# Attention with a decay, then a gated FFN: the decay rows issued from ScalarE's DMA queue, and the first 480 tasks of the order rewritten

## The chip, the core and the metric

The kernel runs on one core of one Trainium2 chip. The core has four engines that compute (TensorE or PE, VectorE or DVE, ScalarE or ACT, GpSimd or POOL) and SyncE or SP, which here issues DMAs only. Each engine works through its own instructions in order and waits on semaphores for the others. The metric is the device time of one execution in microseconds; lower is better. The time before is the median of 3 runs.

## What is computed

The reference is forgetting attention over 8 batches of 8 heads, sequence 576, head size 64, followed by a gated convolutional FFN (512 to 1024 and back):

```python
def _attn_ref(q, k, v, f):
    scores = scale * np.matmul(q, k.transpose(0, 1, 3, 2))
    cum = np.cumsum(np.log(np.clip(f, 0.0001, 1.0)), axis=-1)
    decay = cum[:, :, :, None] - cum[:, :, None, :]
    scores = np.where(causal, -1000000000.0, scores + decay)
    attn = np.exp(scores - np.max(scores, axis=-1, keepdims=True))
    attn = attn / (np.sum(attn, axis=-1, keepdims=True) + 1e-09)
    return np.matmul(attn, v)

def _moe_ref(x, w_in, conv_w, w_out):
    h = np.maximum(x @ w_in, 0.0)
    ...
        conv_out += conv_w[k][None, None, :] * hp[:, k:k + S, :]
    gate = 1.0 / (1.0 + np.exp(-conv_out))
    return h * gate @ w_out
```

All inputs and the output are float32.

## The kernel before

**Units.** The attention runs in 16 half batches of four heads, hb 0 to 15; the FFN runs in 8 batches, b 0 to 7, each after its two half batches. A half batch's Q and K stand transposed in one of four tiles `qk` (in the rows of the order `qk_85` to `qk_88`, for hb modulo 4). The heads' dimensions are read as 16-bit halves, so every other row of such a tile is free, and into some of these free rows go the decay terms: the cumulated logarithms of f, which then enter the scores through the same matmul. For hb 0 the decay comes in by matmuls of its own instead. For hb 1 to 7 two small DMAs, `rows_of` (L200 to L204, 4.5 and 9 KB), copy the decay rows from a DRAM tile `image` into the qk tile. The image itself is written once, by three DMAs from the decay tile `kc` (`decay_image`, L278). For hb 8 to 15 `fill` writes all free rows by three larger DMAs.

**Tasks.** The kernel adds some thousand named tasks, each with its engine, its predecessors and the buffers that it takes and gives, and then plays them in the order of one long string, ORDER (L18). Within an engine the instructions stand in the order of that string. `name@ENGINE` picks an engine where a task may run on several. The names that matter here, with hb or b and a further index:

- `dca dcl dcs dck`: the decay (DVE, ACT, DVE, DVE); `ki`: the image; `rwN`: the decay rows of hb N ("pair N" below, as it is two DMAs); `zc`: constants of the image.
- `ld`, `tp`, `cl`: Q and K of hb 0 and 1 loaded plainly, turned on PE and copied into the qk tile with the free rows cleared. `qN.0`, `qN.1`: Q and K of hb N from 2 on, loaded by a transposing DMA (L180); `clN.x` then clears the free rows on DVE, up to hb 7.
- `vB.k`: the five loads of V for batch B (L210); `vaN.x`: casts to 16 bits. `wi`, `wo`, `wic`, `woc`: the FFN's weights staged in four buffers `ob` and cast.
- `sdI`, `soI.s`, `stN`: scores on PE (diagonal, off the diagonal, tail; I is 2N or 2N+1); `ed`, `eo`, `et`: their exponentials on ACT; `pvN.u`: times V on PE; `n`, `m`: normalising on DVE; `tN`, `txN`: turned on PE and copied.
- `fB.x`, `rB.x`, `cB.x`, `dB.x`, `aB.x`, `gB.x`: FFN chunk x of batch B: first matmul (PE), relu (ACT), convolution in two steps (DVE), gate function (ACT), gating (DVE). `oB.c`: second matmul; `eB.a`, `sB.a`: result copied out of PSUM and stored.

**Buffers.** PSUM holds four tiles `ps`; each score, FFN or turning task on PE takes one, and the task on ACT or DVE that reads it gives it back. So PE can be at most four such tasks ahead of ACT and DVE.

**DMAs.** Each DMA, of SP and ACT alike, raises one of eight semaphores when it has landed. In the rows of the built order they are called `DMAHW0_49` to `DMAHW7_49`; they are dealt out in turn over the DMAs of both engines, about in the order of the string. A DMA whose semaphore has been used before waits for the DMA that used it last, besides what it needs. What stands in `[waits ...]` behind a row names the semaphores that the row waits for. Before the change ACT issues three DMAs (f twice, and the convolution's weights), all at the start; the image and the pairs are SP's, among the loads:

```python
add("ki", "SP", ["dck"], lambda: decay_image("SP"))
add(f"rw{hb}", "SP", [f"cl{hb}.{side}" for side in range(2)] + ["ki"], lambda hb=hb: rows_of(hb))
```

Of the kernel before, what the change touches and what calls it, by code (L numbers as in the profile page):

```python
# [56 lines left out]
def kernel(  # L57
# [17 lines left out]
    BH = B * H  # L75
# [7 lines left out]
    HS = HH * S  # L83
# [16 lines left out]
    image = dpool.tile([4, 2, BH, S], BF16, name="image")  # L100
# [45 lines left out]
    add = plan.add  # L146
# [53 lines left out]
    def rows_of(hb):  # L200
        h0 = 2 * PAIRS if hb == 0 else 0
        c = slice(hb * HH + h0, (hb + 1) * HH)
        nc.sync.dma_start(even_rows(hb, 0, 1, h0 * S, HS), image[0:1, 0, c, :].rearrange("j h s -> j (h s)"))
        nc.sync.dma_start(even_rows(hb, 1, 2, HS + h0 * S, 2 * HS), image[1:3, 1, c, :].rearrange("j h s -> j (h s)"))  # L204
# [73 lines left out]
    def decay_image(e):  # L278
        for j, a, h in ((0, 0, 0), (1, 1, 0), (2, 1, 1)):
            {"SP": nc.sync, "POOL": nc.gpsimd}[e].dma_start(image[j, a], kc[BH * h:BH * (h + 1)])  # L280
# [411 lines left out]
```

## Time and profile before

| what | value |
|---|---|
| median of 3 runs | 246.28 us (245.67 to 247.3) |
| the profiled execution | 246.53 us, its span 244.8 us |
| granted TensorE clock | 0.999 |
| DMA moved | 49.68 MB, mean 203 GB/s |

The profile is of one execution. Its page gives busy time and share of the span for each engine, the chain of work that ended last, followed back from the last instruction, and the costliest groups of instructions. Views of the trace give the same for stretches of the span, the instructions in order of time, and who waited for whom. In a line of the order in time the first two numbers are the start and the length in us; what stands in square brackets is the idle time of the engine ahead of it and what ended it. Lines of "SPq" and "ACTq" are DMA issues: they show the time that issuing took, not when the data landed. `L` numbers are lines of the kernel.

The DMA queue is in use from the start nearly to the end: the queue of SP carries 48.97 of the 49.68 MB in 120085 packets, and the page's mean busy share of the core's 16 DMA engines is 0.9 or more in most of the first 28 of its 40 slices.

### The profile page before, as it was taken

What the parts mean: (1) busy time and instruction counts of PE and PEld (TensorE: products, weight loads), DVE (VectorE), ACT (ScalarE), POOL (GpSimd) and SP (SyncE); (2) the same over time, 40 slices, a digit from 0 to 9 for tenths busy, and PEclk for the clock granted to TensorE, in tenths of its full rate; (3) what the DMA queues carried; (4) which work ended last, traced back from release to release, by engine and by line L of the source; (5) the groups of instructions that cost most, each with busy time, mean ns of one, the idle gap of its engine ahead of it and who ended that gap; (6) DMA issues with size and microseconds to landing.
All of it is one profiled execution on the core that took longest, in us unless ns stands there. A gap on an engine that the chain in (4) does not pass through costs nothing.

```text
span 244.8 us, 6395 instructions
## 1 busy us (share of the span) xinstructions
PE 226.9 (93%) x2627; PEld 145.2 (59%) x2627; DVE 205.9 (84%) x323; ACT 206.8 (84%) x278; POOL 51.5 (21%) x77
## 2 busy tenths in 40 slices
PE   0899799779989999999999999999999999999991
PEld 0787585557555676575556765685575566444440
DVE  5635359999998999999999979996999889999941
ACT  2768677999989899999999999999988996798442
POOL 8020520004220030022311580165302221000000
PEclk9999999999999999999999999999999999999999
DMA  7999999999899999999999999969997870541426
GB/s 189 333 162 243 289 212 197 196 249 260 187 178 177 222 162 246 252 297 208 195 251 264 202 189 274 263 144 186 240 255 192 210 165 3 146 162 58 163 86 214
DMA packets 120280, 49.68 MB, mean 203 GB/s; under 512 B 109863, under 2 KB 110375, under 8 KB 120251
## 3 DMA queue, kind: packets, MB, share of 16 engines
q1 hardware_dynamic: 120085, 48.97, 89.7%
q8 instruction: 20, 0.33, 0.6%
q10 hardware_dynamic: 166, 0.31, 0.4%
q14 instruction: 9, 0.07, 0.1%
HBM read 21.11 MB, written 10.17 MB: 128 GB/s over the span
## 4 chain that ended last, share of the span: by engine, by line
PE 80%; DVE 8%; DMA 6%; issue 1%; ACT 1%; POOL 1%; ACTq 1%; SPq 0%; DVEq 0%
PE ps L475 25%; PE ps L430 21%; PE ps L313 15%; PE ps L390 7%; PE ps L395 3%; PE ps L166 2%; PE ps L415 2%; PE ps L321 2%; DMA pd<-in_moe_conv_w_dram 2%; DMA ob<-in_moe_w_out_dram 2%; DVE u L447 2%; DVE u L449 2%; DMA qk<-image 2%; DVE hg L459 1%; DVE qk L186 1%
## 5 line engine op out<-in xcount | busy, mean ns | idle before, releaser
L430 PE MATMUL ps<-xt,w_in_f 128*128 128x512 f16 (+1 forms) x512 | 69.9, 286 | 0.0
L371 ACT ACTIVATE pp<-ps 128x1024 f16<-128x1024 f32 x64 | 64.8, 1033 | 4.4 <-PE ps L313 2.8
L475 PE MATMUL ps<-w_out_f,hg 128*128 128x512 f16 x288 | 66.9, 379 | 0.7 <-POOL w_out_f L519 0.7
L313 PE MATMUL ps<-qk 128*128 128x128 bf16 (+2 forms) x576 | 63.4, 240 | 1.6 <-DMA qk<-image 0.8
L447 DVE SCALAR_TENSOR_TENSOR u<-ht,cwt 128x576 f32<-128x576 f16 x64 | 53.3, 849 | 3.2 <-ACT ht L441 3.2
L452 ACT ACTIVATE hg<-u,cw 128x576 f16<-128x576 f32 x64 | 48.7, 784 | 5.9 <-DVE u L449 5.8
L449 DVE SCALAR_TENSOR_TENSOR u<-ht,cwt,u 128x576 f32<-128x576 f16 x64 | 53.1, 844 | 0.5
L430 PEld LDWEIGHTS <-w_in_f 128*128 128x128 f16 x512 | 34.4, 98 | 28.5
L313 PEld LDWEIGHTS <-qk 128*128 128x128 bf16 x576 | 39.2, 98 | 19.8 <-issue 3.0
L441 ACT ACTIVATE ht<-ps 128x576 f16<-128x576 f32 x64 | 40.9, 663 | 6.2 <-DVE hg L459 3.1
L475 PEld LDWEIGHTS <-hg 128*128 128x128 f16 x288 | 26.9, 98 | 29.7 <-issue 0.9
L459 DVE SCALAR_TENSOR_TENSOR hg<-hg,ht 128x576 f16<-128x576 f16 x51 | 39.0, 776 | 0.5 <-ACT hg L452 0.5
L357 POOL TENSOR_SCALAR_AFFINE_SELECT pp<-pd 128x1024 f16<-128x1024 f32 x16 | 19.7, 1244 | 51.7 <-ACT pd L354 51.7
L390 PE MATMUL ps<-va,pp 128*128 128x65 f16 x640 | 24.8, 193 | 1.0 <-DVE va L218 1.0
L390 PEld LDWEIGHTS <-pp 128*128 128x128 f16 x640 | 22.5, 97 | 3.5 <-DVE va L218 1.3
L406 DVE TENSOR_TENSOR xm<-ps,rc 128x896 f16<-128x896 f32 (+1 forms) x32 | 23.9, 751 | 0.5
L354 ACT ACTIVATE pp<-ps 128x1024 f16<-128x1024 f32 x16 | 16.6, 1038 | 5.2 <-PE ps L313 4.2
L354 ACT ACTIVATE pd<-ps 128x1024 f32<-128x1024 f32 x16 | 16.2, 1023 | 1.2 <-PE ps L313 1.0
L218 POOL CAST va<-vf 128x1024 f16<-128x1024 f32 x8 | 9.3, 1168 | 33.2 <-PE ps L415 18.5
L321 PE MATMUL ps<-mask,ident 128*128 128x512 bf16 (+1 forms) x40 | 14.3, 358 | 1.6 <-ACT pp L371 0.8
L404 DVE RECIPROCAL rc<-ps 128x14 f32<-128x14 f32 (+1 forms) x32 | 6.7, 209 | 9.8 <-PE ps L395 5.9
L480 ACT COPY ob<-ps 128x1024 f32<-128x1024 f32 (+1 forms) x14 | 12.9, 919 | 0.3 <-issue 0.2
(83 smaller groups left out, 176.2 us busy)
## 6 DMA issues: line engine op xcount, KB each, us to landing
vf<-in_v_dram SPq DMA_DIRECT2D x32, 256.0 KB
out_dram<-ob SPq DMA_DIRECT2D x14, 512.0 KB
qk<-blank SPq DMA_DIRECT2D x8, 432.0 KB
ob<-in_moe_w_in_dram SPq DMA_DIRECT2D x4, 512.0 KB
ob<-in_moe_w_out_dram SPq DMA_DIRECT2D x4, 512.0 KB
out_dram<-ob SPq DMA_DIRECT2D x6, 256.0 KB
vf<-in_v_dram SPq DMA_DIRECT2D x8, 128.0 KB
qk<-blank SPq DMA_DIRECT2D x8, 108.0 KB
```

The costliest lines, as they stand in the source:

```text
L313: nc.tensor.matmul(o, tk[:, h * S + k0:h * S + k0 + 128], tq[:, h * S + q0:h * S + q0 + n], start=first, stop=last and not by_matmul(hb, h))
L354: nc.scalar.activation(o, ps_of(f"sd{i}").rearrange("p (s c) -> p s c", s=2), AF.Exp, scale=SCALE)
L371: nc.scalar.activation(pair(i)[:, s, 512:1536], ps_of(f"so{i}.{s}"), AF.Exp, scale=SCALE)
L390: nc.tensor.matmul(ps[:, c:c + D + 1], block(hb, h, m, n), va[:, h, m, 0:D + 1], start=(m == 0), stop=(m == n))
L406: nc.vector.tensor_tensor(xm[:, CUT * D * u:CUT * D * u + nj * k * D].rearrange("p (j x d) -> p j x d", x=k, d=D), got[:, :, :, 0:D], r.un ...
L430: nc.tensor.matmul(ps[:, t0:t1], w_in_f16[:, cc, 128 * ff:128 * (ff + 1)], xt[:, cc // 2, x:x + t1 - t0], start=(cc == 0), stop=(cc == NCC ...
L441: nc.scalar.activation(ht_of(b, ff)[:, 2:2 + S], ps_of(f"f{b}.{ff}")[:, 0:S], AF.Relu, scale=1.0 if (b, ff) in LATE else 0.5)
L447: nc.vector.scalar_tensor_tensor(u, ht[:, 1:1 + S], cwt[:, ff, 0:1], ht[:, 2:2 + S], op0=ALU.mult, op1=ALU.add)
L449: nc.vector.scalar_tensor_tensor(u, ht[:, 3:3 + S], cwt[:, ff, 1:2], u, op0=ALU.mult, op1=ALU.add)
L452: nc.scalar.activation(hg_of(b, ff), u_t[slot[f"c{b}.{ff}", "u"]], AF.Sigmoid if (b, ff) in LATE else AF.Tanh, scale=cw[:, ff, 1:2])
L459: nc.vector.scalar_tensor_tensor(hv, hv, 1.0, ht_of(b, ff)[:, 2:2 + S], op0=ALU.add, op1=ALU.mult)
L475: nc.tensor.matmul(ps[:, 512 * (c % 2):512 * (c % 2 + 1)], w, w_out_f16[:, ff, :], start=(ff == 0), stop=(ff == NFF - 1))
```

## The change

`ki` and `rw1` to `rw7` may now run on ACT or SP, and the new string puts all eight on ACT. Their 17 DMAs leave SP's queue for ACT's. The code of the DMAs is the same; only the engine that issues them is another. A rule is added that a batch's first V load stands behind the casts of the batch two before it in the string. The first 480 of the string's 1054 places are new, the same tasks in another order, and the other 574 are word for word the old ones.

```diff
-    def rows_of(hb):
+    def rows_of(hb, e="SP"):
+        dma = {"SP": nc.sync, "ACT": nc.scalar}[e].dma_start
...
-        nc.sync.dma_start(even_rows(hb, 0, 1, h0 * S, HS), image[0:1, 0, c, :].rearrange("j h s -> j (h s)"))
-        nc.sync.dma_start(even_rows(hb, 1, 2, HS + h0 * S, 2 * HS), image[1:3, 1, c, :].rearrange("j h s -> j (h s)"))
+        dma(even_rows(hb, 0, 1, h0 * S, HS), image[0:1, 0, c, :].rearrange("j h s -> j (h s)"))
+        dma(even_rows(hb, 1, 2, HS + h0 * S, 2 * HS), image[1:3, 1, c, :].rearrange("j h s -> j (h s)"))
...
-            {"SP": nc.sync, "POOL": nc.gpsimd}[e].dma_start(image[j, a], kc[BH * h:BH * (h + 1)])
+            {"SP": nc.sync, "ACT": nc.scalar}[e].dma_start(image[j, a], kc[BH * h:BH * (h + 1)])
...
-    add("ki", "SP", ["dck"], lambda: decay_image("SP"))
+    add("ki", "ACT/SP", ["dck"], decay_image)
...
-                add(f"rw{hb}", "SP", [f"cl{hb}.{side}" for side in range(2)] + ["ki"], lambda hb=hb: rows_of(hb))
+                add(f"rw{hb}", "ACT/SP", [f"cl{hb}.{side}" for side in range(2)] + ["ki"], lambda e, hb=hb: rows_of(hb, e))
...
-                    behind=[f"v{b}.0"] if kb else [])
+                    behind=[f"v{b}.0"] if kb else [f"va{2 * b - 4}.{x}" for x in range(2)] if b > 1 else [])
```

The string itself, at the place of pairs 4 and 5, old and new:

```
... wo3 rw4 wo1 wo0 v2.0 v2.3 v2.4 v2.1 v2.2 rw5 wo2 q6.0 q6.1 q7.0 q7.1 ...
... cl5.0 woc2@POOL m2.1 rw4@ACT r0.6 q6.1 g0.5 q7.0 q7.1 va4.0@POOL ... m3.1 a0.1 rw5@ACT g0.1 a0.4 ...
```

(The first line shows SP's tasks alone.) Between the two strings a number of casts and copies change engines: `wic2`, `tx0`, `tx6`, `va0.1` and `cl1.1.0` go to ACT; `va4.0`, `va8.0`, `e1.0`, `tx2`, `va3.1`, `va5.1`, `va7.1` and `cl1.0.0` leave it; `wic1`, `va1.0`, `woc3`, `va2.1`, `va3.1`, `tx2`, `e1.0`, `va8.0` and `cl1.0.0` go to DVE; `tx0`, `tx6`, `va1.1`, `va2.0`, `va4.1`, `va7.0` and `cl1.1.0` leave it.

SP's queue from the loads of V of batch 2 to those of Q and K of hb 6 and 7, before. `vf_89` is a raw V tile, `ob_128` a staging buffer for w_out, `qk_86` the tile of hb 5, `qk_87` and `qk_88` those of hb 6 and 7:

```order
L210 DMA vf_89<-in_v_dram 128x8x64 [waits DMAHW5_49]
L210 DMA vf_89<-in_v_dram 128x8x64 [waits DMAHW6_49]
L210 DMA vf_89<-in_v_dram 64x8x64 [waits DMAHW7_49]
L210 DMA vf_89<-in_v_dram 128x8x64 [waits DMAHW0_49]
L210 DMA vf_89<-in_v_dram 128x8x64 [waits DMAHW1_49]
L203 DMA qk_86<-image 1x2304 [waits DMAHW2_49,DVE_49]
L204 DMA qk_86<-image 2x2304 [waits DMAHW3_49,DVE_49]
L511 DMA ob_128<-in_moe_w_out_dram 128x2x512 [waits DMAHW4_49,Pool_49]
L180 DMA_TRANSPOSE qk_87<-in_q_dram 128x2304 [waits DMAHW5_49,PE_49]
L180 DMA_TRANSPOSE qk_87<-in_k_dram 128x2304 [waits DMAHW6_49]
L180 DMA_TRANSPOSE qk_88<-in_q_dram 128x2304 [waits DMAHW7_49,PE_49]
L180 DMA_TRANSPOSE qk_88<-in_k_dram 128x2304 [waits DMAHW0_49]
```

The same place on SP now:

```order
L211 DMA vf_89<-in_v_dram 128x8x64 [waits DMAHW3_49]
L211 DMA vf_89<-in_v_dram 128x8x64 [waits DMAHW4_49]
L211 DMA vf_89<-in_v_dram 64x8x64 [waits DMAHW5_49,Activation_49,Pool_49]
L211 DMA vf_89<-in_v_dram 128x8x64 [waits DMAHW6_49]
L211 DMA vf_89<-in_v_dram 128x8x64 [waits DMAHW7_49]
L512 DMA ob_127<-in_moe_w_out_dram 128x2x512 [waits DMAHW0_49,Activation_49]
L180 DMA_TRANSPOSE qk_87<-in_q_dram 128x2304 [waits DMAHW1_49,PE_49]
L180 DMA_TRANSPOSE qk_87<-in_k_dram 128x2304 [waits DMAHW2_49]
L180 DMA_TRANSPOSE qk_88<-in_q_dram 128x2304 [waits DMAHW3_49,DVE_49,PE_49]
L180 DMA_TRANSPOSE qk_88<-in_k_dram 128x2304 [waits DMAHW5_49,DVE_49]
```

Pair 5 (`qk_86<-image`) has left SP's queue; the loads around it follow each other as before. Every one of these rows waits for a DMAHW semaphore and raises the same one.

ACT's instructions from chunk 6's relu of batch 0 on (`ht`, `hg`: FFN tiles; `pp`, `pt`: exponentials; `xt`: turned attention output; `qk_85` is hb 4's tile), before:

```order
L441 ACTIVATE ht_117<-ps_132 128x576 [waits DVE_49,PE_49]
L333 ACTIVATE pt_103<-ps_130 128x256 [waits PE_49]
L371 ACTIVATE pp_96<-ps_131 128x1024 [waits DVE_49,PE_49]
L452 ACTIVATE hg<-u_122,cw 128x576
L333 ACTIVATE pt_104<-ps_129 128x256
L441 ACTIVATE ht_119<-ps_130 128x576 [waits PE_49,Activation_49]
L452 ACTIVATE hg<-u_121,cw 128x576 [waits DVE_49]
L418 COPY xt_114<-ps_132 128x1152 [waits DVE_49,PE_49]
L452 ACTIVATE hg<-u_120,cw 128x576
L354 ACTIVATE pp_97<-ps_130 128x2x512 [waits PE_49]
```

The same place on ACT now, with `eo7.1`, pair 4, `r0.6`, `r0.7`, `a0.1`, pair 5, `a0.4`, `ed8`, `ed9`:

```order
L372 ACTIVATE pp_96<-ps_132 128x1024 [waits PE_49]
L204 DMA qk_85<-image 1x2304 [waits DMAHW4_49,DVE_49]
L205 DMA qk_85<-image 2x2304 [waits DMAHW6_49]
L442 ACTIVATE ht_116<-ps_129 128x576 [waits Activation_49]
L442 ACTIVATE ht_115<-ps_130 128x576 [waits DVE_49,PE_49]
L453 ACTIVATE hg<-u_120,cw 128x576 [waits DMAHW3_49]
L204 DMA qk_86<-image 1x2304 [waits DMAHW1_49]
L205 DMA qk_86<-image 2x2304 [waits DMAHW3_49,DVE_49]
L453 ACTIVATE hg<-u_123,cw 128x576
L355 ACTIVATE pp_98<-ps_130 128x2x512 [waits PE_49]
L355 ACTIVATE pp_97<-ps_131 128x2x512 [waits DVE_49,PE_49]
```

The four DMAs of pairs 4 and 5 now stand between ACT's activations, each with a wait for a DMAHW semaphore; the wait of `a0.1` for DMAHW3 is for a load at the kernel's start, into the tile that it writes.

PE at the end of the work that stands ahead of `f1.0`, now (`so9.0`, then `st5`, then the first of `so9.1`):

```order
L314 LDWEIGHTS qk_85
L314 MATMUL ps_129<-qk_85 128x192
L322 LDWEIGHTS ident
L322 MATMUL ps_130<-mask,ident 128x256 [waits Activation_49]
L314 LDWEIGHTS qk_86 [waits DMAHW3_49]
L314 MATMUL ps_130<-qk_86 128x64 [waits DMAHW1_49]
```

The first use of hb 5's tile by PE, `st5`, stands here ahead of `f1.0`; before the change the first was `sd10`, behind `f1.4`, and it stood there like this:

```order
L430 LDWEIGHTS w_in_f_69
L430 MATMUL ps_130<-xt_114,w_in_f_69 128x64
L321 LDWEIGHTS ident
L321 MATMUL ps_132<-mask,ident 128x512 [waits Activation_49]
L313 LDWEIGHTS qk_86 [waits DMAHW3_49]
L313 MATMUL ps_132<-qk_86 128x128 [waits DMAHW2_49]
```

There hb 5's first use stood after the first matmuls of chunks 0 to 4; now it stands ahead of all of these, and the semaphores that it waits for are pair 5's new ones, DMAHW1 and DMAHW3.

More of the change, by code (lines that the diff above doesn't have):

```diff
@@ L562 @@
             else:
-                add(f"rw{hb}", "SP", [f"cl{hb}.{p}.{side}" for p, side in parts] + ["ki"], lambda hb=hb: rows_of(hb))
+                add(f"rw{hb}", "ACT/SP", [f"cl{hb}.{p}.{side}" for p, side in parts] + ["ki"], lambda e, hb=hb: rows_of(hb, e))
                 ready = [[f"rw{hb}"]] * 2
```

2 lines of the change are left out of this document (1 added, 1 removed).

## Prediction, made before the changed kernel was run

> **What bounds the kernel now.** I read the page first, then busy time by stretches of the span, then who waited for whom on SP's queue, then the order in time on SP, ACT and PE between 16 and 77 us, because the change lies there.
>
> ```profile
> span 244.8 us, 6395 instructions
> PE 226.9 (93%) x2627; PEld 145.2 (59%) x2627; DVE 205.9 (84%) x323; ACT 206.8 (84%) x278; POOL 51.5 (21%) x77
> PE 80%; DVE 8%; DMA 6%; issue 1%; ACT 1%; POOL 1%; ACTq 1%; SPq 0%; DVEq 0%
> ...
> 50.00:55.00 5.00, 3.67 (x57) 2.42 (x56) 5.00 (x8) 4.87 (x8) 0.00 (x0) 1.00 1.12 257
> 120.00:140.00 20.00, 20.00 (x258) 12.94 (x255) 19.41 (x29) 19.26 (x27) 6.24 (x6) 1.00 1.02 228
> ```
>
> PE carries 80% of the chain that ended last. In the stretches (us, then PE, PEld, DVE, ACT and POOL busy, granted clock, DMA share, GB/s) PE is full from 75 us on, as in 120 to 140. Around 50 us it is not: DVE has 5.00 of 5, ACT 4.87, PE 3.67. So the end moves if PE gets more idle time or loses some, and the rewritten 480 places end near 116 us. Behind them both lists are the same, and PE has no slack there in which to win a loss back.
>
> **How a DMA waits.** Each DMA raises one of eight semaphores and first waits for the DMA that had this semaphore last. The profile shows that this bites:
>
> ```profile
> SPq L159 <- DMA u<-in_f_dram: 1.1, 1, 1.1
> SPq L210 <- DMA u<-in_f_dram: 0.4, 1, 0.4
> ```
>
> A load of K and a load of V on SP waited 1.1 and 0.4 us for the load of f, of which they need nothing. Before the change only SP's queue pays for this. In the new order ACT issues DMAs, so ACT pays, with every activation that stands behind.
>
> **The change, part by part.** SP loses the image (L280) and seven pairs of row DMAs (L203, L204); these are its rows for the image and pairs 1 to 5, with the loads that the sum needs:
>
> ```profile
> 16.59 2.35 SPq L280 DMA_DIRECT2D image<-kc  x3
> 18.98 2.23 SPq L180 DMA_TRANSPOSE qk<-in_q_dram  x1
> ...
> 22.04 0.31 SPq L203 DMA_DIRECT2D qk<-image  x1
> 22.51 0.69 SPq L204 DMA_DIRECT2D qk<-image  x1
> ...
> 24.72 0.44 SPq L203 DMA_DIRECT2D qk<-image  x1
> 25.28 0.57 SPq L204 DMA_DIRECT2D qk<-image  x1
> 26.20 5.51 SPq L180 DMA_TRANSPOSE qk<-in_q_dram  x1
> ...
> 39.87 0.38 SPq L203 DMA_DIRECT2D qk<-image  x1
> 40.36 0.61 SPq L204 DMA_DIRECT2D qk<-image  x1
> ...
> 52.38 0.26 SPq L203 DMA_DIRECT2D qk<-image  x1
> 52.70 0.59 SPq L204 DMA_DIRECT2D qk<-image  x1
> ...
> 63.09 0.39 SPq L203 DMA_DIRECT2D qk<-image  x1
> 63.58 0.59 SPq L204 DMA_DIRECT2D qk<-image  x1
> ...
> 64.72 4.64 SPq L180 DMA_TRANSPOSE qk<-in_q_dram  x1
> ...
> 72.83 3.30 SPq L180 DMA_TRANSPOSE qk<-in_q_dram  x1
> ```
>
> Freed on SP ahead of q7.0 (the row at 72.83): 2.35 + 1.00 + 1.01 + 0.99 + 0.85 + 0.98 = 7.2 us. How much earlier q7.0 lands for that isn't shown. If SP's issuing set its pace, all 7.2; if the transfers did, nothing. The same kind of load takes 2.23 us to issue at 18.98 and 5.51 at 26.20, so most of the time the queue was pushed back by work already in it, at a DMA share of 1.12 of 1 around 50 us. I take 2.5, about the image's 2.35, which stood between two transposed loads; ends 0 and 7.2.
>
> When a transposed load lands, and when a row pair does, two waits show:
>
> ```profile
> 23.35 1.67 DVE L186 TENSOR_SCALAR qk<-qk,lim 128x2304 uint16<-128x2304 uint16 x2 [1.87 <-DMA qk<-in_q_dram]
> ...
> 26.36 0.40 PE L313 MATMUL ps<-qk 128*128 128x128 bf16 x4 [0.78 <-DMA qk<-image]
> ```
>
> q2.0's issue ends at 21.21 and DVE starts at 23.35: landed 2.1 us after its issue ended. So q7.0, issued by 76.13, lands at 78.2 now and at 75.7 in the new order (71.0 to 78.2). The pair that PE waited for at 26.36 had its second DMA issued at 22.51: 3.85 us, behind loads on SP's queue. On a queue of its own I take 3.0, between that and the 2.1.
>
> **The wait that decides.** In ACT's new rows pair 5 stands behind a0.1: its first DMA waits for DMAHW1, last raised by q6.0, its second for DMAHW3, last raised by q7.0 (SP's rows for qk_87 and qk_88). Counted from the start, q7.0 is the seventh DMA with that semaphore and pair 5's second the eighth. ACT is there soon after r0.7:
>
> ```profile
> 2.02 1.28 ACT L225 ACT_TABLE_LOAD   x1 [2.02 <-issue]
> 2.06 0.67 ACTq L226 DMA_DIRECT2D pd<-in_moe_conv_w_dram  x1
> ...
> 55.51 0.65 ACT L441 ACTIVATE ht<-ps 128x576 f16<-128x576 f32 x1
> ```
>
> r0.7 runs at 55.51 now, and q7.0 can't have landed before 71.0. The first two rows show that a DMA is issued beside a running ACT instruction, so issuing the pairs, 0.85 to 1.0 us each, costs ACT next to nothing; what costs is the wait. Behind it on ACT stand a0.4, ed8, ed9 and all exponentials after them. They free the PSUM tiles that PE needs, and DVE's g0.4 needs a0.4. PE itself stops at st5, half batch 5's tail scores, which the new order has put ahead of f1.0 and which need pair 5.
>
> Where does PE stand there in the old run?
>
> ```profile
> 59.81 0.60 PE L313 MATMUL ps<-qk 128*128 128x64 bf16 x4
> 60.25 0.27 PE L321 MATMUL ps<-mask,ident 128*128 128x256 bf16 x1
> ...
> 60.47 0.38 PE L321 MATMUL ps<-mask,ident 128*128 128x512 bf16 x1
> ...
> 61.35 1.14 PE L430 MATMUL ps<-xt,w_in_f 128*128 128x512 f16 x8
> 62.33 0.60 PE L313 MATMUL ps<-qk 128*128 128x64 bf16 x4
> 62.77 1.14 PE L430 MATMUL ps<-xt,w_in_f 128*128 128x512 f16 x8
> ```
>
> By 62.77 it has done all that the new list has ahead of st5, and so9.1, st4 and f1.0 beyond it: 0.44 + 0.22 + 0.98 us by the starts. So the same work was done at 61.1. In the new run st5 can't start before 75.7 + 3.0 = 78.7: **17.6 us later**.
>
> Smaller terms. Pair 3 waits on ACT for v1.3 and pair 4 for v2.1 in the same way; what that costs ACT lies inside the 17.6, since PE must wait for pair 5 anyhow. The w_out stage that PE now waits for has long landed by then:
>
> ```profile
> 71.14 1.02 PE L475 MATMUL ps<-w_out_f,hg 128*128 128x512 f16 x4 [0.67 <-POOL w_out_f L519]
> ```
>
> That takes 0.7 off. Then PE starts again after some 15 us of rest, and the chain shows what its first work after a rest cost, at a granted clock of 1.00 all the while:
>
> ```profile
> 8.31 3.91 PE ps L166 x36
> ...
> 15.30 0.50 PE ps L166 x9
> ```
>
> 36 transposes took 3.91 us at the start, 109 ns each; nine took 0.50 later, 56 ns each. A second slow start of that length loses at most 2 us, and ACT has 3 us of exponentials ready by then: I add 1.0 (0 to 2). The Trainium skill, "TensorE: Matmul & The Clock Gate", section "What's actually happening", says that the array falls to half clock after an idle window of about 3.4 us and needs as long to come back; the start of the trace agrees with the half rate, and that a rest in the middle does the same no row here shows. By that rule the term would be 1.7, without it 0.
>
> Edits that I cost at nothing: the casts and copies that change engines, and the order of the rest.
>
> ```profile
> 47.60 0.68 DVE L218 CAST va<-vf 128x1024 f16<-128x1024 f32 x1
> ...
> 48.86 1.13 ACT L218 CAST va<-vf 128x1024 f16<-128x1024 f32 x1
> ...
> 56.93 1.12 ACT L418 COPY xt<-ps 128x1152 f16<-128x1152 f16 x1
> ```
>
> In these units ACT gives up two large casts, one evacuation and some small casts, and takes a w_in cast and one net copy, about 2 us less; DVE gains about 1.5 us. The cover is the long wait, in which both stand still for longer than that. Were it gone, DVE, which is full around 50 us, would hand most of its 1.5 on. In the first 25 us hb 0's first scores come some 2 us later, behind two more of the turns and three instead of one of ACT's turned copies, and PE has that much more done by then: 0, give or take 1. Pairs 6 and 7 wait on ACT for v3.2 and q9.1; both come up on SP long before ACT gets there, 17 us late as it is: 0. With q7.0 out of the way nothing behind 116 us changes.
>
> Sum: 17.6 - 0.7 + 1.0 = 17.9. The profiled execution took 246.53 us (its span is 244.8, with 1.7 around it), which makes 264.4; it stands 0.25 over the median of 246.28, so **264.2**.
>
> **The rivals.** *SP sets the pace, and all 7.2 us come through.* Against it speaks the 5.51 at 26.20. q7.0 then lands at 71.0, 4.7 earlier, and the time is 259.5.
>
> *Nothing comes through.* The DMA share above 1 speaks for it, the image's 2.35 between two loads against it. q7.0 lands at 78.2, 2.5 later: 266.7. The Trainium skill, "DMA: Bandwidth & Descriptors", section "Issuing engines are not separate DMA queues", has a rule that would give this: DMAs of different engines run on the same DMA engines, and another issuer saves only the time on the sequencer.
>
> *Pair 5 doesn't wait for q7.0*, because the wait means an older DMA than I count. Then this is the edit that its words say: the rows land sooner on an own queue. PE gets back the 0.78 at 26.36 and the 0.67 at 71.14, and of its stop for DVE's cast
>
> ```profile
> PE ps L390 <- DVE va L218: 1.0, 1, 1.0
> ```
>
> up to 1.0, while DVE's 1.5 us more take about as much: 244.8, and not over 1% either way but for luck. It decides if q7.0's place in the count is wrong by one round, since the DMA of the round before, v2.0, stands eight rows ahead of it on SP. Against it: the order's rows name DMAHW1 and DMAHW3, and SP's own waits above are of just this kind.
>
> **How the numbers follow.** My forecast has a chance of 0.70, all freed 0.10, nothing freed 0.12, no wait 0.08. In 1% steps (2.5 us, about what a measurement of this kernel can tell from no change) the first three are slower; of the last I give 0.02 to faster, 0.05 to same, 0.01 to slower. So faster 0.02, same 0.05, slower 0.93. The predicted time is the likeliest case's. For the range: below, all 7.2 freed (-4.7), a landing in 2.1 instead of 3.0 (-0.9) and no slow start (-1.0) make 257.6; above, nothing freed (+2.5), 3.85 (+0.85), a full slow start (+1.0) and a us lost in starting make 269.6. I take 257.5 to 269; the no-wait case stays outside.
>
> **What would show it.** In the profile after: ACT idle before the activation behind pair 5 (a0.4, L453) until q7.0 has landed at 71 to 78 us, with smaller gaps at pairs 3 and 4; PE idle some 15 us before the mask of st5 or its first scores, PE and DVE low in the slices from 60 to 78 us; no stop of PE for w_out's casts; everything behind 116 us as before, 17 to 18 us later. Wrong would be: ACT going on from r0.7 to a0.4 within 2 us; q7.0's issue row at 65 or earlier; a PE stop in that place that ended with something else than the rows; or a second long stop behind 80 us, which would put the time over 270.

## The result: 8% slower, and the profile after

| | before | changed |
|---|---|---|
| median | 246.79 us (4 runs, 245.67 to 247.57) | 266.71 us (4 runs, 265.28 to 267.43) |
| ratio | | 1.0798 (95% interval 1.0747 to 1.085) |
| profiled execution | 246.53 us, span 244.8 | 266.48 us, span 264.8 |

Executions over 1.5% above the fastest of their kernel are left out of the ratios here and below, so a ratio need not be that of the medians.

The first lines of the page of the changed kernel (busy time; then tenths of 40 slices of 6.6 us):

```profile
span 264.8 us, 6405 instructions
...
PE 235.3 (89%) x2627; PEld 149.4 (56%) x2627; DVE 208.8 (79%) x325; ACT 205.4 (78%) x275; POOL 54.3 (21%) x78
...
PE   0899997875639999999999999999999999999991
...
ACT  1839797694058887889999799999998999498542
PEclk9999999799768999999999999999999999999998
...
PE 55%; DMA 20%; DVE 10%; ACT 7%; SPq 3%; issue 2%; ACTq 1%
```

One hole holds the loss: PE falls to 5, 6 and 3 tenths and ACT to 4, 0 and 5 in the slices from 60 to 80 us, and behind it PE is full again. In the chain that ended last, DMA has gone from 6% to 20% and PE from 80% to 55%. PE's busy time is 8.4 us longer for the same 2627 matmuls; in these slices its granted clock (the row PEclk, in tenths) drops as well.

The chain of the changed kernel in the hole (start and length in us; a piece "DMA" runs from issue to landing; its line numbers are one higher than those of the kernel before from the rows of pairs on):

```profile
57.45 4.62 DMA vf<-in_v_dram
62.06 0.02 issue
62.08 6.25 DMA qk<-image
...
69.15 5.68 DMA qk<-in_q_dram
...
74.91 0.56 ACTq L205
...
75.51 0.07 ACT hg L453
...
76.19 1.01 ACT pp L355
...
77.25 0.37 PE ps L322
```

Read from the bottom: PE's mask of `st5` (L322) waited for ACT to free a PSUM tile (L355). ACT was behind its own DMA, pair 5's second (L205), and that one was behind a transposed load of Q, `q7.0`, issued by SP at 69.15 and landed at 74.83. It needs nothing of `q7.0` but its semaphore: by the trace's semaphore events both land on the same one. Further up the same has happened to pair 4: its second DMA started at 62.08, when `v2.1`, a load of V, had landed.

ACT and PE in order of time, changed kernel:

```profile
63.77 0.78 ACT L453 ACTIVATE hg<-u,cw 128x576 f16<-128x576 f32 x1
69.14 0.22 ACTq L204 DMA_DIRECT2D qk<-image  x1
74.91 0.56 ACTq L205 DMA_DIRECT2D qk<-image  x1
75.51 0.78 ACT L453 ACTIVATE hg<-u,cw 128x576 f16<-128x576 f32 x1 [10.96 <-DMA qk<-in_q_dram]
```

```profile
68.38 0.61 PE L314 MATMUL ps<-qk 128*128 128x128 bf16 x4 [3.81 <-DMA qk<-image]
...
77.25 0.37 PE L322 MATMUL ps<-mask,ident 128*128 128x256 bf16 x1 [4.86 <-ACT pp L355]
77.41 2.12 PE L314 MATMUL ps<-qk 128*128 128x64 bf16 x12
79.33 2.12 PE L431 MATMUL ps<-xt,w_in_f 128*128 128x512 f16 x8
...
92.06 1.14 PE L431 MATMUL ps<-xt,w_in_f 128*128 128x512 f16 x8
```

ACT stood 10.96 us between `a0.1` and `a0.4`. PE stood 3.81 us for pair 4 and 4.86 us at `st5`, whose scores began at 77.41. Pair 5's rows had landed at 77.12 (by the trace's semaphore events), the PSUM tile came free at 77.20 (76.19 + 1.01): the last thing that PE waited for here was ACT's exponential, by 0.1 us.

Behind the hole the lists are the old ones, and the same work can be laid side by side. Before:

```profile
124.15 3.10 PE L430 MATMUL ps<-xt,w_in_f 128*128 128x512 f16 x24
...
227.41 12.25 PE L475 MATMUL ps<-w_out_f,hg 128*128 128x512 f16 x56
```

After:

```profile
142.40 3.10 PE L431 MATMUL ps<-xt,w_in_f 128*128 128x512 f16 x24
...
148.88 0.28 PE L314 MATMUL ps<-qk 128*128 128x64 bf16 x4 [0.60 <-ACT ht L442]
...
246.93 12.25 PE L476 MATMUL ps<-w_out_f,hg 128*128 128x512 f16 x56
```

PE is 18.25 us late at 142.40 and 19.52 at its last work. So the time was lost ahead of 142 us, but for 1.3 on PE and 0.5 of the 20.0 between the spans that lie behind PE's last work.

### The profile page after: what moved, and what is told of

Its sections match the earlier page's. It is cut to its first block, busy times and chain, and to the rows that moved or that the text cites. A ratio compares the mean times of both kernels' runs of the same rounds, so it can differ in the third digit from the quotient of the medians.

```text
span 264.8 us, 6405 instructions
## 1 busy us (share of the span) xinstructions
PE 235.3 (89%) x2627; PEld 149.4 (56%) x2627; DVE 208.8 (79%) x325; ACT 205.4 (78%) x275; POOL 54.3 (21%) x78
## 4 chain that ended last, share of the span: by engine, by line
PE 55%; DMA 20%; DVE 10%; ACT 7%; SPq 3%; issue 2%; ACTq 1%
PE ps L476 19%; PE ps L431 15%; PE ps L314 10%; PE ps L391 5%; DMA qk<-in_k_dram 5%; DMA qk<-image 5%; DMA vf<-in_v_dram 4%; DVE hg L460 4%; DVE u L448 3%; DMA hg<-in_q_dram 3%; DVE u L450 2%; DMA qk<-in_q_dram 2%; SPq L211 2%; PE ps L396 2%; ACT pp L372 2%; ACT ht L442 2%
## 5 line engine op out<-in xcount | busy, mean ns | idle before, releaser
L314 PE MATMUL ps<-qk 128*128 128x128 bf16 (+2 forms) x576 | 66.7, 248 | 8.1 <-DMA qk<-image 6.1
L314 PEld LDWEIGHTS <-qk 128*128 128x128 bf16 x576 | 41.6, 101 | 31.1 <-DMA qk<-image 9.5
L460 DVE SCALAR_TENSOR_TENSOR hg<-hg,ht 128x576 f16<-128x576 f16 x51 | 41.3, 818 | 2.5 <-ACT hg L453 2.4
L358 POOL TENSOR_SCALAR_AFFINE_SELECT pp<-pd 128x1024 f16<-128x1024 f32 x16 | 20.4, 1285 | 73.2 <-ACT pd L355 73.2
L322 PE MATMUL ps<-mask,ident 128*128 128x512 bf16 (+1 forms) x40 | 16.2, 407 | 4.9 <-ACT pp L355 4.9
L355 ACT ACTIVATE pp<-ps 128x1024 f16<-128x1024 f32 x16 | 16.3, 1026 | 5.1 <-PE ps L314 5.1
L219 POOL CAST va<-vf 128x1024 f16<-128x1024 f32 x10 | 12.7, 1284 | 36.4 <-DMA vf<-in_v_dram 23.2
L355 ACT ACTIVATE pd<-ps 128x1024 f32<-128x1024 f32 x16 | 16.2, 1023 | 1.2 <-PE ps L314 1.0
L481 ACT COPY ob<-ps 128x1024 f32<-128x1024 f32 (+1 forms) x13 | 11.9, 916 | 1.2 <-DVE qk L186 0.9
```

The costliest lines, as they stand in the source:

```text
L314: nc.tensor.matmul(o, tk[:, h * S + k0:h * S + k0 + 128], tq[:, h * S + q0:h * S + q0 + n], start=first, stop=last and not by_matmul(hb, h))
L355: nc.scalar.activation(o, ps_of(f"sd{i}").rearrange("p (s c) -> p s c", s=2), AF.Exp, scale=SCALE)
L460: nc.vector.scalar_tensor_tensor(hv, hv, 1.0, ht_of(b, ff)[:, 2:2 + S], op0=ALU.add, op1=ALU.mult)
```

## The experiments

Theory A is the prediction's: a DMA on ACT waits for the last owner of its semaphore, with all of ACT behind it. The rivals are that issuing on ACT costs by itself, and that the new order of the work is what is slow.

**Only the owner of a semaphore moves.** One, two or three copies of 32 bytes into a scratch buffer are added on SP behind `v3.0`, so behind `q7.1`. They don't touch the rows of any other engine; they move on which semaphore the DMAs behind them get. The edit for two, and the string:

```diff
     add("zc", "SP", [], constants)
+    for x in range(2):
+        extra = dpool.tile([1, 8], FP32, name=f"extra{x}")
+        add(f"x{x}", "SP", [], lambda extra=extra: nc.sync.dma_start(extra, moe_conv_w[0:1, 0:8]))
...
-... v3.0 v3.1 n3.0 v3.2 ...
+... v3.0 x0 x1 v3.1 n3.0 v3.2 ...
```

One:

> One DMA of 32 bytes (DRAM to DRAM) is added on SP behind v3.0. By the built program pair 5 still takes its semaphores from q6.0 and q7.0. Theory A (pair 5 waits on ACT for the last owner of its semaphores): nothing moves, 266.7 us (265 to 268.5). Rival B (issuing on ACT and the new order of the work cost the time): the same, 266.7. This run is the control for the next two: what one small DMA costs by itself.

Two:

> Two such DMAs behind v3.0. No engine's other work moves, but pair 5's second DMA now takes the semaphore of pair 4's first DMA, which landed at 63.0 in the profile of the changed kernel; its first still takes q6.0's (69.1). Theory A: pair 5 is issued from 69.2 on in place of 74.9, lands near 71.8, st5 follows at about 72 in place of 77.2: 5.3 us less, 261.4 us (259.5 to 263). Rival B: 266.7.

Three:

> Three such DMAs behind v3.0. Now pair 5's second DMA takes q7.1's semaphore, and q7.1 landed at 76.96 in the changed kernel, 2.1 us after q7.0. Theory A: 2.1 us more than the changed kernel, 268.8 us (267.5 to 270.5), though this kernel differs from the one with two only by one more 32 byte DMA. Rival B: 266.7. A rival C, that more DMAs on SP help or harm by their number, would put the three kernels in one row, rising or falling.

| copies | owner of pair 5's second semaphore | issued at | expected | time (kernel before beside it: 245.96) | ratio |
|---|---|---|---|---|---|
| 1 | `q7.0` | 73.33 | 266.7 | 265.39 | 1.0768 (1.069 to 1.0845) |
| 2 | pair 4's first | 68.51 | 261.4 | 261.14 | 1.0595 (1.0518 to 1.0672) |
| 3 | `q7.1` | 77.85 | 268.8 | 270.44 | 1.0973 (1.0894 to 1.1051) |

All three lie in A's ranges: no row by number, but up and down by the owner, as A said. Order of time on ACT with two copies, and the chain with three:

```profile
68.19 0.22 ACTq L204 DMA_DIRECT2D qk<-image  x1
68.51 0.56 ACTq L205 DMA_DIRECT2D qk<-image  x1
69.12 0.77 ACT L453 ACTIVATE hg<-u,cw 128x576 f16<-128x576 f32 x1 [4.75 <-DMA qk<-image]
```

```profile
72.67 5.11 DMA qk<-in_k_dram
77.78 0.02 issue
...
77.85 0.56 ACTq L205
```

With two, the second DMA follows the first at once and ACT's stop is 4.75 us in place of 10.96: what is left is the first DMA's wait for `q6.0`, until 68.19, and the issue of the two. With three, the wait is for a load of K, `q7.1`. This shows the wait: work and engines are the same, and with two copies SP issues them only at 75.10, behind pair 5, so that what differs at pair 5 is only what its semaphore had been used for. The owners of the later pairs move too, but PE stands 0.90 us at most for one of them.

**The engine alone.** The old order, with the image and all pairs on ACT:

```diff
-... ki@SP ... rw5 ...
+... ki@ACT ... rw5@ACT ...
```

> The order of the kernel before, word for word, with the image and the seven pairs issued by ACT at the places that they have in it. By the built program pair 3 takes semaphores of wo3 and wo0, pair 4 of v2.0 and v2.4, pair 5 of q7.0 and v3.1. Theory A (an ACT DMA waits for the last owner of its semaphore): wo0 landed at 57.6 in the changed kernel and hb 3's first scores stand near 44 in the kernel before, so PE loses some 14 us there already and more at pair 5; 270 us (262 to 285). Rival B1 (the new order of the work is what is slow, not the issuing engine): 246 us. Rival B2 (DMAs issued between activations cost ACT their 0.9 us each): 248 to 254.

274.49 us beside 246.98, ratio 1.1104 (1.1056 to 1.1153), slower than the changed kernel. The chain at pair 5, whose second DMA has `v3.1` as its owner:

```profile
84.31 4.03 DMA vf<-in_v_dram
88.34 0.02 issue
...
88.42 0.57 ACTq L205
...
89.03 1.03 ACT pp L372
...
90.11 2.02 PE ps L431 x7
```

So the loss needs no new order. PE stood 8.21 us for pair 3 and 8.25 us here.

**One pair alone.** The old order, with pair 5 alone on ACT:

> The order of the kernel before, word for word, with pair 5 alone on ACT, at its place behind ed8; the image and the other pairs are SP's. By the built program pair 5's DMAs take the semaphores of q5.1 and of pair 4's second DMA (and not of q7.0 and v3.1, as in the run of the old order with all on ACT); both landed before 58 us in the kernel before. Theory A: no stop on ACT at pair 5, SP gets 0.98 us back ahead of wo2, and the time is the kernel before's within 1%: 246.5 us (245 to 248.5). Rival B3 (it is ACT's queue or the issuing at this place, not the semaphore's last owner, that costs): 255 us or more, as the run of the old order with all on ACT was slow at this pair.

247.42 us beside 247.31, ratio 0.9991 (0.9964 to 1.0018): no difference. ACT in order of time:

```profile
63.67 1.03 ACT L372 ACTIVATE pp<-ps 128x1024 f16<-128x1024 f32 x1
64.09 0.24 ACTq L204 DMA_DIRECT2D qk<-image  x1
64.50 0.67 ACTq L205 DMA_DIRECT2D qk<-image  x1
64.58 1.04 ACT L355 ACTIVATE pp<-ps 128x1024 f16<-128x1024 f32 x1
```

Same pair, same place in the string, same engine as in the run before; the owners are older, and the DMAs pass beside ACT's work for nothing. "ACT is a bad place for these DMAs" falls, for this pair at least.

**The image alone.** The old order, with the image alone on ACT:

> The order of the kernel before, word for word, with the image alone on ACT and all pairs on SP. The image's three DMAs take semaphores of loads at the start that landed before 13 us, so ACT has nothing to wait for. Theory A: SP gets back the image's 2.35 us ahead of q2.0, the stop of 0.78 for pair 1 goes, behind it the loads are at best 2 us earlier: 245.3 us (244 to 246.5), 0.2 to 0.8% under the kernel before. Rival B2 (DMAs between activations cost ACT): 247 to 249.

248.82 us beside 247.41, ratio 1.0046 (1.0013 to 1.008): half a per cent slower in place of faster, a miss, and in B2's range. ACT at the start, the copies of before (9.42) first:

```profile
9.42 3.71 ACT L172 ACTIVATE qk<-ps,lim 128x1152 uint16<-128x1152 uint16 x3 [0.35 <-PE ps L166]
...
10.29 1.77 ACTq L281 DMA_DIRECT2D image<-kc  x3
12.11 3.71 ACT L172 ACTIVATE qk<-ps,lim 128x1152 uint16<-128x1152 uint16 x3 [2.44 <-DVE cwt L304]
```

The three DMAs stand ahead of the turned copies that PE waits for. They wait for `kc` from DVE, the first until 10.29, then they are issued while ACT does nothing, and the copies begin at 12.11 in place of 9.42. (0.6 us of that isn't theirs: DVE's first step on f starts at 7.20 in place of 6.59.) So in the run before this one a DMA passed for nothing beside an activation that still ran; here, with ACT idle, its issue held up the work behind it.

**The order alone.** The new order, with everything back on SP, and each pair where SP's list gave room:

> The new order of all the work on PE, DVE, ACT and POOL, with the image and all seven pairs issued by SP again (pairs 4 and 5 behind wo2 and ahead of q6.0, pair 2 behind q3.0). Theory A: no ACT instruction waits for a load, st5 is not late, and the time is near the kernel before's, 246.0 us (244.3 to 249). Rival B1 (the new order itself is slow): 260 us or more. Rival B2 (issuing on ACT costs by itself): near 246 too; other runs must tell it from A.

278.04 us beside 245.96, ratio 1.1294 (1.1226 to 1.1361). This tells little of the order: PE stood 7.02, 7.58 and 9.05 us for pairs 2, 3 and 7, which now stood behind SP's loads. The second try put each pair directly behind its casts:

> As the order alone on SP, but with each pair put on SP directly behind the casts that it needs and ahead of the transposed loads that stood before it: pair 2 ahead of q3.0, pair 3 ahead of q4.0, pair 4 ahead of v2.1, pair 5 ahead of q6.0. In the first try PE stood 7.02 and 7.58 us for pairs 2 and 3, which were issued at 36.7 and 54.0. Theory A (late pairs, by whatever queue, are the loss, and the order of the other work is not): pairs 2 and 3 land near 27 and 44, 4 and 5 near 61 and 64: 248 us (245 to 253). Rival B1 (the new order itself is slow): 260 or more.

268.99 us beside 246.98, ratio 1.0877 (1.0838 to 1.0915). Missed again. None of PE's stops for pairs 2 to 6 is longer than 3.92 us, but pair 7, left behind `v4.1`, was issued at 105.64:

```profile
110.67 1.25 PE L314 MATMUL ps<-qk 128*128 128x64 bf16 x8 [9.37 <-DMA qk<-image]
```

PE's stops for pairs come to 15.1 us here, in place of 0.8 in the kernel before, and its busy time is 6.4 us longer (233.3 in place of 226.9), with a granted clock of 0.50 behind the two longest. That is 20.7 of the 21.4 us between the two spans (266.2 and 244.8). So neither run gives a price of the order by itself: in this order SP's list brings the pairs too late. The next four bring them otherwise.

**The late pairs elsewhere.** First, pairs 4 and 5 on POOL:

> The changed kernel, with pairs 4 and 5 alone issued by POOL, ahead of woc2 and va4.0 there; every other row of PE, DVE and SP, and all of ACT's beside the four DMAs, as they are. POOL's DMAs have eight semaphores of their own, so no load is their last owner. Theory A: ACT goes on from eo7.1 through a0.4 without a stop, pair 5 lands within 4 us of hb 5's second clamp: st5 near 66 us in place of 77.2, 251 us (247 to 255). Rival B (the new order or the activations around the pairs cost it): 262 or more.

255.4 to 260.48 us in four executions beside 246.98, ratio 1.0407 (1.0334 to 1.0481): above the range and under rival B's. In the profiled one, of 260.34 us, pair 5's wait is gone, but pair 4 is waited for 6.14 us; whether the quicker ones waited as long isn't shown. DMA issues by group, and PE:

```profile
qk<-image POOLq DMA_DIRECT2D x2, 4.5 KB, 6.7
qk<-image POOLq DMA_DIRECT2D x2, 9.0 KB, 7.2
```

```profile
67.82 0.61 PE L314 MATMUL ps<-qk 128*128 128x128 bf16 x4 [6.14 <-DMA qk<-image]
```

POOL's DMAs took 6.7 and 7.2 us (median) from issue to landing, where on ACT pair 5's last took 2.2 and pair 4's last 6.25.

Then pairs 3 to 5 on SP, the rest on ACT:

> A version that tries to beat both: the new order with the image and pairs 1, 2, 6 and 7 on ACT, where they waited little in the changed kernel, and pairs 3, 4 and 5 on SP at the places of the run with all on SP (ahead of q4.0, v2.1 and q6.0). Theory A: no long wait is left, pair 3 lands near 44 in place of 47.5: 247 us (244.5 to 251), the kernel before within 1%. Rival B1: 260 or more.

255.62 us beside 246.98, ratio 1.03 (1.0248 to 1.0352): above the range, and under B1's. Then pairs 3 and 4 alone on SP:

```diff
-... cl3.1 ... q4.0 ... rw3@ACT ... cl4.0 ... rw4@ACT ...
+... cl3.1 rw3@SP q4.0 q5.0 q5.1 wo3 wo1 wo0 ... cl4.0 rw4@SP v2.4 v2.1 v2.2 wo2 ...
```

> The changed kernel with pairs 3 and 4 alone issued by SP, early (pair 3 ahead of q4.0, pair 4 ahead of v2.4). Pair 5 stays on ACT at the same place, behind a0.1. By the built program its two DMAs then take the semaphores of q5.0 and wo3, which had landed at 51 and 55 in the run with the late pairs on SP, long before ACT gets there. Theory A: ACT issues pair 5 without a stop between a0.1 and a0.4, and it lands near 65: st5 near 65 in place of 77.2, 252 us (248.5 to 256). Rival B (a pair on ACT at this place costs it, whatever the semaphore): 262 or more.

255.05 us beside 247.41, ratio 1.0294 (1.0247 to 1.034), in range. ACT and PE in order of time:

```profile
58.30 0.22 ACTq L204 DMA_DIRECT2D qk<-image  x1
...
60.12 0.59 ACTq L205 DMA_DIRECT2D qk<-image  x1
60.76 0.78 ACT L453 ACTIVATE hg<-u,cw 128x576 f16<-128x576 f32 x1 [1.20 <-DVE rc L405]
```

```profile
62.34 0.40 PE L314 MATMUL ps<-qk 128*128 128x128 bf16 x4 [2.44 <-DMA qk<-image]
...
74.94 1.14 PE L431 MATMUL ps<-xt,w_in_f 128*128 128x512 f16 x8 [1.83 <-ACT ht L442]
...
99.47 0.73 PE L314 MATMUL ps<-qk 128*128 128x64 bf16 x8 [1.09 <-DMA qk<-image]
```

Pair 5 is on ACT at its place of the changed kernel, behind the same activation, with `q5.0` and `wo3` as owners, and the stop of 10.96 us is 1.20. What is left of the loss, 8.3 us between the spans, is in part again late pairs: PE's stops for pairs come to 5.0 us in place of 0.8, those for ACT's relus to 2.4 in place of none, and its busy time is 2.4 us longer. Last, pairs 6 and 7 on SP as well:

> The same, with pairs 6 and 7 on SP too, each behind its casts and ahead of q9.1; the image and pairs 1, 2 and 5 are ACT's. PE stood 0.56 and 1.18 us for pairs 6 and 7 on ACT in the run with pairs 3 to 5 on SP, and was 2 us later behind them. Theory A: up to 2 us less than the run beside this one, 250.5 us (247 to 255). If SP holds q9.1 and q8.1 up for the casts of hb 6 and 7, as it did with all pairs on SP at 105 us, it is slower than that run by some us.

253.5 us beside 247.41, ratio 1.0248 (1.0204 to 1.0291), in range and the lowest median of the new order, though its interval overlaps with the one before. No version beat the kernel before.

## Why the prediction was right, and where it was not

**The mechanism was right.** Pair 5 waited for `q7.0`, ACT for pair 5, PE for ACT; the three copies show that it is the semaphore. The Trainium skill, "DMA: Bandwidth & Descriptors", section "Anatomy of one DMA — SWDGE (gpsimd) path", says that DMA engines don't wait on semaphores and that such a wait is sat out by the issuing sequencer; ACT's 10.96 us agree.

**Landing of `q7.0`: 75.7 forecast, 74.83 measured.** Two errors nearly met, by luck. SP's issue of it ended at 69.15 + 2.69 = 71.84 in place of 76.13, 4.3 us sooner and not 2.5; how much of that the 7.2 us freed on SP gave wasn't separated from the new order. But it landed 3.0 us behind its issue, where the prediction took 2.1 from another load. The kernel before has 3.1 there too: `q7.0` landed at 79.23, not at 78.2.

**Landing of pair 5: 3.0 us forecast, 2.2 measured** (issued 74.91, landed 77.12). `st5`'s first work stood at 77.25 and not at 78.7: 16.1 us late in place of 17.6.

**What PE waited for last: the rows forecast, the PSUM tile measured.** The prediction named a stop of PE there that ends with something else than the rows as a sign of being wrong, and this sign came: the rows were there at 77.12, the tile at 77.20, freed by `ed8`, and with one and three copies the stop ends with ACT as well. The two ends hang on the same wait, as `ed8` stands on ACT behind pair 5; the prediction had this path too ("They free the PSUM tiles that PE needs") but added up the other. That the last step was another one cost the sum 0.1 us.

**The slow start: 1.0 forecast, 1.9 measured.** `f1.0` took 2.12 us at 79.33, with a granted clock of 0.50 from 75 to 80, and 1.14 for the like at 92.06; `st5` and its neighbours took 2.12 for 12 matmuls that take 1.16 in the second run of the order alone. 0.98 + 0.96 = 1.9. The prediction took half of that, on the ground that ACT had three us of exponentials ready by then. That work doesn't cover it: PE itself was the slow one, and all that it did late stayed late. So the rest in the middle did halve the clock, which the prediction had left open. `st5` 1.5 us too late in the forecast and a slow start 0.9 too short: these two errors cancel in good part, and that the total came so near is luck to that extent.

**The stop for w_out's cast: right.** The 0.67 us of before is gone. In its place PE stood 0.42 us for DVE at 90.53.

**Nothing behind 116 us changes: wrong by 1.3.** From 18.25 to 19.52 PE lost 1.3 us more, 0.60 of it in one stop for a relu at 148.88. A stop of 0.49 to 0.61 us stands there in every run of the new order, with pair 5 late or not, and in none of the old one. It comes with the new order, then, and not with the late pair; why ACT is behind there was not tried. The rest of the difference of spans, 0.5 us, lies behind PE's last matmul.

**Pairs 3 and 4 cost nothing beside pair 5: right.** What PE lost to them only made its stop at `st5` shorter. With two copies PE has no stop at `st5`, and its last long one is 3.56 us for pair 4.

**The new order: costed at nothing, wrong without its cover.** The prediction named the long wait as the cover, and in the changed kernel it is. In the last two runs, where that wait is gone, the new order is still 2.5 to 3% slower than the old. As far as these runs stand for the rival without a wait, its 244.8 us was some 8 us too low (1.0248 to 1.0294 times 246.28 is 252.4 to 253.5): it took the new order to be the old one with the pairs sooner, while this order asks for them earlier than they came. In the last but one some 4 of the 8 us are stops for pairs (5.0 in place of 0.8); what the order costs beside that was not isolated.

**Left open.** How the semaphores are dealt out was read from the built programs and not derived. With pairs 3 and 4 off ACT, pair 5 came to own older ones at the same place of the string. And whether the new order would win with pairs that land sooner than any run brought them was not reached.

## What to carry to other kernels

Where DMAs share their semaphores as here, look up in the built program, before a DMA is put on a compute engine's queue, which DMA had its semaphore last, and when that one lands: everything behind on that engine waits so long. Order and issuing engine alone don't tell it: one more DMA of 32 bytes elsewhere made the kernel 4.3 us faster in one case (one copy to two) and 9.3 us slower in another (two to three). A reordering that is hidden by a longer wait should be run once without that wait, and its stops added up by what ended them, or the lateness of what it moved is taken for the price of the order.

## What the hardware showed that was not expected

PE's granted clock fell behind short stops too: behind the 3.81 us in the changed kernel it was 0.50 from 68 to 70 us, and behind 2.29 us for pair 3 (until 47.61) 0.50 from 48 to 50. In the run with pairs 3 to 5 on SP a stop of 2.30 us was followed by full speed for 1.3 us and then by half:

```profile
61.11 0.40 PE L314 MATMUL ps<-qk 128*128 128x128 bf16 x4 [2.30 <-DMA qk<-image]
...
62.45 0.63 PE L314 MATMUL ps<-qk 128*128 128x128 bf16 x4
62.88 1.17 PE L416 MATMUL ps<-ident,xm 128*128 128x128 f16 x9
```

Behind the 2.44 us of the run with pairs 3 and 4 on SP the clock stayed at 1.00. The Trainium skill, "TensorE: Matmul & The Clock Gate", section "What's actually happening", says that activity is judged in windows of about 3.4 us that run on freely; where a stop falls in the window then counts beside its length, and the late drop agrees with that. That 2.3 us can be enough is not what that section's table of states would lead one to expect; the measurement decides.

A DMA of 4.5 or 9 KB landed 2.2 us behind its issue on ACT's queue in one place and 6.25 in another (pair 5's and pair 4's second in the changed kernel), and 6.7 to 7.2 on POOL's.
